# Subtracting the low parts of the first layer's converted weights on GpSimd instead of VectorE

## The chip, the cores and the metric

The kernel runs on one core of one Trainium2 chip. The metric is the device time of one execution in microseconds; the median of several executions is given. A core has five engines with a queue of their own each, and each queue is worked off in order: PE (TensorE, the matrix products), DVE (VectorE), ACT (ScalarE), POOL (GpSimd) and SP (SyncE, which here only issues DMAs). They wait for one another by semaphores. In the profile PEld stands for PE's weight loads.

## The reference

Three parts follow one another, all in float32:

```python
# 1: linear attention, q k v of (8, 8, 576, 64)
q_s = exp(q - max(q, -1)); q_s /= sum(q_s, -1) + 1e-9
k_s = exp(k - max(k, 2));  k_s /= sum(k_s, 2) + 1e-9
x = q_s @ (k_s^T @ v)                    # heads joined: 4608 x 512
# 2: first layer, moe_w_in 512 x 2048, moe_w_out 2048 x 512
x = (relu(x @ moe_w_in) ** 2) @ moe_w_out
# 3: second layer, moe2_w_in and moe2_w_out of the same shapes
h = x @ moe2_w_in
x = where(h > 0, h, exp(min(h, 0)) - 1) @ moe2_w_out
```

## The kernel before

**Split operands.** PE multiplies values of a rounded float type. To keep float32 accuracy each operand is split into a high part (the value, rounded) and a low part (the value minus its high part), and each product is made as three: high by high, high by low and low by high. For a weight tile of the first layer, the high part is made on ACT (`w_hi`, L133) and the low part is the subtraction of L143 (`w_lo`) on DVE.

**Conversion of the weights.** The weights come in as 64-bit words holding the float32 pairs and are taken apart by `w_scale` (two ACT instructions, L105 and L106) and put together by two bit operations on DVE, `w_fields` (L111) and `w_sign` (L116), into a tile `mt`, of which there are two. `w_hi` and `w_lo` then read `mt`. Each of these five steps works on one chunk, 128 x 512. The first layer has 32 chunks: wi0, tile 0 to 15, and wo0, tile 0 to 15, in the order in which they are used (the list `early`). Their high and low parts stay in SBUF (`resident` is true) in the tiles wi0h, wi0l and wo. The chunks of the second layer's wo1 are converted by the same functions with `resident` false, much later, and go to DRAM.

**Blocks.** The 4608 tokens are worked off in nine blocks of 512. Block 0 runs while the weights are converted: for each of the 16 tiles j, `up` (L544 to L546) makes twelve products for ph, ACT makes relu and square, ACT and DVE split the result into gh and gl (`up_split`, L565 on DVE), and `down` (L576 to L578) makes twelve products for y, two tiles behind. After each `up` come two calls of `convert(s, steps)`, one for each of 32 steps s. A call emits, in this order: `w_scale` for chunks up to s + 4; a third of the attention steps prepared for this s; `w_lo` up to chunk s + 1; a second third; `w_hi` up to s + 2 and `w_fields` up to s + 3; the last third; `w_sign` up to s + 3; and the load up to s + 8. The first three chunks' `w_lo` are emitted in `first_block`, which does the attention of block 0 in an order written out by hand.

**The attention steps beside it.** In the 32 steps of block 0 the attention of block 1 is done: for each of four pairs of heads, `k_max` (L259), `k_sub` (L272, one operand in PSUM), the exponential on ACT, `kv_mm` (the product pk, L286) and small sums on DVE; for each of four token tiles q, `q_max`, `q_sub` (L332), the exponential, `q_sum` and `q_norm` (L366). `x_tr` (L379) then transposes q on PE, and `x_mm` (L400) makes the block's input.

**POOL.** Its queue holds in these steps the memsets of the ones beside v (`v_load`, L249 and L250; vr has two buffers, so each waits for the pk product two pairs before) and of kvs (`kv_mm`, L295). Later it issues the DMAs that write the sums of the weights to DRAM (L199, L206, L211) and wo1's parts (L135, L145).

**Order.** All instructions are emitted in the order written in the code; nothing is reordered between emission and queue. The first layer's other eight blocks run in pairs with fewer products (L661, on sums of the weights prepared while blocks 1 and 2 run), and the second layer after them (L816, L877 to L879).

Of the kernel before, what the change touches and what calls it, by code (L numbers as in the profile page):

```python
# [13 lines left out]
ALU = mybir.AluOpType  # L14
# [6 lines left out]
def tile_attention_moe_moe2(  # L21
# [18 lines left out]
    nc = tc.nc  # L40
# [34 lines left out]
    def f32(ap):  # L75
        return ap.bitcast(F32)
# [3 lines left out]
    raw, mid, spill = {}, {}, {}  # L80
# [56 lines left out]
    def w_lo(w, j, resident):  # L137
        if resident:
            hi, lo = wh[w, j], wl[w, j]
        else:  # L140
            hi = spill.pop((w, j))
            lo = pool.tile([P, DM], F32R, tag="st", bufs=4, name=f"sl_{w}_{j}")
        nc.vector.tensor_tensor(lo, f32(mid.pop((w, j))), f32(hi), op=ALU.subtract)  # L143
        if not resident:
            nc.gpsimd.dma_start(w2d[w, j][:, 1, :], f32(lo))  # L145

# [322 lines left out]
    def first_block():  # L469
# [34 lines left out]
        for i, f in ((201, w_scale), (222, w_fields), (225, w_sign), (244, w_hi), (266, w_lo)):  # L504
            for c in range(-(-(325 - i) // 28)):
                put(i + 28 * c, chunk, f, c)
# [7 lines left out]
    def chunk(f, *cs):  # L514

        for c in cs:
            if 0 <= c < len(early) and (f, c) not in done:
                done.add((f, c))
                f(*early[c], *((True,) if f in (w_hi, w_lo) else ()))

    def convert(s, steps):


        i, j = len(steps) // 3, 2 * len(steps) // 3
        chunk(w_scale, *range(s + 5))
        run(steps[:i])
        chunk(w_lo, *range(s + 2))
        run(steps[i:j])
        chunk(w_hi, *range(s + 3))
        chunk(w_fields, *range(s + 4))  # L530
        run(steps[j:])
        chunk(w_sign, *range(s + 4))
        chunk(w_load, *range(s + 9))
# [728 lines left out]
```

## Time and profile before

| what | value |
|---|---|
| median of 3 timed runs | 1619.68 us (1619.37 to 1620.75) |
| span of the profiled execution | 1615.5 us |
| PE busy | 1586.3 us, 98% |
| DVE busy | 1051.3 us, 65% |
| ACT busy | 974.7 us, 60% |
| POOL busy | 90.6 us, 6% |
| granted clock of TensorE | 1.000, mean of the span |

The profile is of one execution. Its own time is the span from the first to the last instruction; the timed runs also hold what lies around it. Busy is the time in which an engine had an instruction under way; instructions of one engine can overlap at their ends, so a duration can be longer than the distance to the next start. The page's shares are means over the whole span; a change that touches one stage is read in the rows of that stage.

### The profile page before, as it was taken

The numbers are of one execution on the slowest core, as the hardware profiler recorded it, in microseconds if no ns is written. First come the engines' busy times: TensorE is split into PE (matmuls) and PEld (weight loads), VectorE is DVE, ScalarE is ACT, GpSimd is POOL, SyncE is SP. The second block draws the span as 40 slices with busy tenths as digits, with TensorE's granted clock in tenths as the row PEclk, the third lists the DMA queues.
The fourth block names the chain that finished last, engine by engine and source line by source line (L and its number), as shares of the span: only waits on it lengthen the run. The fifth ranks groups of instructions, "written<-read, shape, count | busy, mean of one in ns | idle before, by whom it ended". The sixth has DMA issues, their size and how long they took to land.

```text
span 1615.5 us, 22809 instructions
## 1 busy us (share of the span) xinstructions
PE 1586.3 (98%) x7958; PEld 1350.8 (84%) x7958; DVE 1051.3 (65%) x1658; ACT 974.7 (60%) x1665; POOL 90.6 (6%) x222
## 2 busy tenths in 40 slices
PE   6999999999999999999999999999999999999999
PEld 4778778878788787887888998998989999898997
DVE  7987596777877686773677554555545555555544
ACT  7996655566555675556556655555555565555544
POOL 0001220012101220011000000000000000000000
PEclk9999999999999999999999999999999999999999
DMA  7747566667775685653587555435534543543531
GB/s 264 258 156 246 197 216 198 204 210 237 257 226 174 219 289 164 201 196 111 181 288 259 197 194 173 150 110 154 171 106 143 172 129 117 190 125 109 172 112 59
DMA packets 163953, 296.17 MB, mean 183 GB/s; under 512 B 16384, under 2 KB 52224, under 8 KB 163840
## 3 DMA queue, kind: packets, MB, share of 16 engines
q1 hardware_dynamic: 154240, 263.25, 51.4%
q0 software_dynamic: 9600, 31.46, 4.9%
q8 instruction: 64, 1.05, 0.3%
q14 instruction: 49, 0.40, 0.1%
HBM read 238.03 MB, written 56.62 MB: 182 GB/s over the span
## 4 chain that ended last, share of the span: by engine, by line
PE 82%; DVE 8%; issue 5%; ACT 2%; DMA 2%; POOL 1%; SPq 1%; POOLq 0%; DVEq 0%; ACTq 0%
PE p L816 22%; PE p L661 18%; PE y L878 8%; PE y L879 8%; PE y L877 8%; PE ph L544 5%; PE ph L546 5%; PE ph L545 5%; PE px L400 2%; DVE ks L272 1%; PE pt L379 1%; PE pk L286 1%; DVE mt_wi L111 1%; DVE mt_wi L116 1%; POOL w1s L199 1%
## 5 line engine op out<-in xcount | busy, mean ns | idle before, releaser
L816 PE MATMUL p<-x2h,w 128*128 128x384 f32 x1344 | 359.6, 337 | 0.0
L661 PE MATMUL p<-uh,w 128*128 128x512 f32 x896 | 282.5, 392 | 2.9 <-DMA w<-w1s 2.9
L816 PEld LDWEIGHTS p<-x2h,w 128*128 128x128 f32 x1344 | 245.0, 188 | 4.4 <-ACT h L916 0.2
L544 PE MATMUL ph<-xh,wi0h 128*128 128x512 f32 x576 | 230.7, 401 | 0.1
L879 PE MATMUL y<-wo,g2l 128*128 128x512 f32 x576 | 226.0, 392 | 0.0
L878 PE MATMUL y<-wo,g2h 128*128 128x512 f32 x576 | 225.7, 392 | 0.0
L816 PE MATMUL p<-x2l,w 128*128 128x384 f32 x672 | 225.6, 336 | 0.0
L546 PE MATMUL ph<-xh,wi0l 128*128 128x512 f32 x576 | 225.0, 391 | 0.2 <-DVE wi0l L143 0.2
L545 PE MATMUL ph<-xl,wi0h 128*128 128x512 f32 x576 | 224.4, 390 | 0.0
L877 PE MATMUL y<-wo,g2h 128*128 128x512 f32 x576 | 224.0, 389 | 0.0
L661 PEld LDWEIGHTS p<-uh,w 128*128 128x128 f32 x896 | 168.2, 188 | 38.5 <-ACT uh L648 1.9
L918 DVE TENSOR_TENSOR h<-p,p 128x384 f32<-128x384 f32 x144 | 79.6, 553 | 183.1 <-PE p L816 181.9
L648 ACT ACTIVATE uh<-B 128x512 fp32r<-128x512 f32 x192 | 121.2, 632 | 109.4 <-PE p L661 63.7
L908 ACT ACTIVATE p<-p 128x384 f32<-128x384 f32 x144 | 69.9, 486 | 187.2 <-PE p L816 187.2
L649 DVE TENSOR_TENSOR ul<-B,uh 128x512 fp32r<-128x512 f32 x192 | 131.2, 690 | 69.3 <-ACT uh L648 68.3
L661 PE MATMUL p<-ul,w 128*128 128x512 f32 x448 | 175.3, 391 | 0.2
L553 ACT ACTIVATE B<-ph 128x512 f32<-128x512 f32 x128 | 76.2, 595 | 117.0 <-PE ph L546 116.4
L816 PEld LDWEIGHTS p<-x2l,w 128*128 128x128 f32 x672 | 126.2, 188 | 3.9
L544 PEld LDWEIGHTS ph<-xh,wi0h 128*128 128x128 f32 x576 | 109.2, 189 | 23.1 <-issue 0.9
L546 PEld LDWEIGHTS ph<-xh,wi0l 128*128 128x128 f32 x576 | 108.1, 188 | 24.1 <-DVE wi0l L143 1.1
L545 PEld LDWEIGHTS ph<-xl,wi0h 128*128 128x128 f32 x576 | 108.3, 188 | 22.8 <-issue 0.7
L879 PEld LDWEIGHTS y<-wo,g2l 128*128 128x128 f32 x576 | 108.1, 188 | 22.8
(127 smaller groups left out, 2372.1 us busy)
## 6 DMA issues: line engine op xcount, KB each, us to landing
w<-w2s SPq DMA_DIRECT2D x336, 256.0 KB, 3.0
w<-w1s SPq DMA_DIRECT2D x224, 256.0 KB, 3.4
raw_wi<-wi_dram SPq DMA_DIRECT2D x32, 512.0 KB, 4.2
raw_wo<-wo_dram SPq DMA_DIRECT2D x32, 512.0 KB, 4.0
ks<-k_dram SPq DMA_DIRECT2D x32, 320.0 KB, 4.7
vr<-v_dram SPq DMA_DIRECT2D x32, 320.0 KB, 5.6
kt<-kt_dram SPq DMA_DIRECT2D x32, 288.0 KB, 3.8
q<-q_dram SPq DMA_DIRECT2D x36, 256.0 KB, 4.7
```

What stands on the lines that cost most here:

```text
L544: nc.tensor.matmul(ph, hi[:, c], xh[p], start=(p == 0), stop=False)
L545: nc.tensor.matmul(ph, hi[:, c], xl[p], start=False, stop=False)
L546: nc.tensor.matmul(ph, lo[:, c], xh[p], start=False, stop=(p == NP - 1))
L553: nc.scalar.activation(g, ph, AF.Relu)
L648: nc.scalar.activation(hi, x, AF.Copy)
L649: nc.vector.tensor_tensor(lo, x, f32(hi), op=ALU.subtract)
L661: nc.tensor.matmul(accs[side, m], w[:, s, m], x, start=(new and (j, s) == (0, 0) and x is hi), stop=(j == NG - 1 and s == 1), skip_group_c ...
L816: nc.tensor.matmul(acc, w[:, s, k], x[:, k], start=(begin and (k, s) == (0, 0) and x is hi), stop=((k, s) == (1, 1)), skip_group_check=not ...
L877: nc.tensor.matmul(y2[c], gh[:, cs], hi, start=first, stop=False)
L878: nc.tensor.matmul(y2[c], gh[:, cs], lo, start=False, stop=False)
L879: nc.tensor.matmul(y2[c], gl[:, cs], hi, start=False, stop=last)
L918: nc.vector.tensor_tensor(h, part[add], part["bank", i], op=ALU.add)
```

## The change

In `w_lo` the subtraction goes to GpSimd where the parts are resident, which are the 32 chunks of wi0 and wo0, and stays on DVE for wo1's. Operands, tiles, their buffers and the place in the order of emission are the same.

```diff
@@ -140,7 +140,8 @@
         else:
             hi = spill.pop((w, j))
             lo = pool.tile([P, DM], F32R, tag="st", bufs=4, name=f"sl_{w}_{j}")
-        nc.vector.tensor_tensor(lo, f32(mid.pop((w, j))), f32(hi), op=ALU.subtract)
+        eng = nc.gpsimd if resident else nc.vector
+        eng.tensor_tensor(lo, f32(mid.pop((w, j))), f32(hi), op=ALU.subtract)
         if not resident:
             nc.gpsimd.dma_start(w2d[w, j][:, 1, :], f32(lo))
```

## Rows read from the trace of the kernel before

**Rows 1.** The page's first line: span and instructions.

```profile
span 1615.5 us, 22809 instructions
```

**Rows 2.** Instructions of L143: ns min/median/max, first and last start us, shapes.

```profile
L143 DVE TENSOR_TENSOR wi0l<-mt_wi,wi0h x16: 643/684/687, 25.2 to 115.8; 128x512 fp32r<-128x512 f32 x16
L143 DVE TENSOR_TENSOR wo<-mt_wo,wo x16: 679/685/692, 37.8 to 127.5; 128x512 fp32r<-128x512 f32 x16
```

**Rows 3.** Stretches: length, busy (count) of PE, PEld, DVE, ACT, POOL, clock, DMA share, GB/s.

```profile
41.00:61.00 20.00, 19.81 (x102) 15.40 (x101) 19.83 (x35) 18.89 (x36) 0.27 (x3) 1.00 0.73 257
61.00:81.00 20.00, 19.29 (x100) 15.05 (x100) 19.77 (x40) 17.82 (x35) 0.42 (x4) 1.00 0.75 254
81.00:101.00 20.00, 16.95 (x108) 13.32 (x106) 19.53 (x40) 18.76 (x37) 0.00 (x0) 1.00 0.44 145
101.00:121.00 20.00, 19.56 (x92) 15.86 (x93) 15.27 (x26) 18.80 (x36) 0.00 (x0) 1.00 0.48 166
...
140.00:238.00 98.00, 97.47 (x554) 78.54 (x554) 75.12 (x164) 62.19 (x121) 24.19 (x54) 1.00 0.69 237
```

**Rows 4.** Chain of waits, 20 to 145 us: start, length, engine, output, line.

```profile
59.83 0.61 DVE wi0l L143
...
61.80 0.69 DVE wo L143
...
65.55 0.60 DVE wi0l L143
...
68.81 0.60 DVE wo L143
...
100.78 0.61 DVE q L366
101.44 0.33 PE pt L379
```

**Rows 5.** DVE's groups, 41 to 101 us: busy us, mean ns, idle before.

```profile
L116 DVE SCALAR_TENSOR_TENSOR mt_wi<-raw_wi,mt_wi 128x512 int32<-128x512 int32 x10 | 6.9, 687 | 0.1
...
L143 DVE TENSOR_TENSOR wo<-mt_wo,wo 128x512 fp32r<-128x512 f32 x10 | 6.9, 686 | 0.0
L565 DVE TENSOR_TENSOR gl<-g,gh 128x512 fp32r<-128x512 f32 x10 | 6.9, 685 | 0.3 <-ACT gh L563 0.3
...
L143 DVE TENSOR_TENSOR wi0l<-mt_wi,wi0h 128x512 fp32r<-128x512 f32 x10 | 6.8, 680 | 0.0
L272 DVE TENSOR_TENSOR ks<-ks,pm 128x512 f32<-128x512 f32 (+1 forms) x8 | 3.5, 480 | 0.1
L366 DVE TENSOR_TENSOR q<-q,qz 128x512 f32<-128x512 f32 x4 | 2.7, 685 | 0.0
...
L353 DVE TENSOR_REDUCE qz<-q 128x8 f32<-128x512 f32 x4 | 2.7, 677 | 0.0
L259 DVE TENSOR_REDUCE km<-kt 128x1 f32<-128x576 f32 x3 | 2.2, 747 | 0.0
L327 DVE TENSOR_REDUCE qm<-q 128x8 f32<-128x512 f32 x3 | 2.0, 681 | 0.0
L362 DVE RECIPROCAL qz<-qz 128x8 f32<-128x8 f32 x4 | 0.8, 196 | 0.0
```

**Rows 6.** POOL's groups over the whole span, columns as in rows 5.

```profile
L295 POOL MEMSET kvs<- 128x128 f32 x32 | 6.7, 217 | 9.5 <-PE px L400 9.5
...
L249 POOL MEMSET vr<- 128x5 f32 x32 | 3.7, 118 | 175.7 <-PE pk L286 127.1 <-issue 48.6
...
masks.py:199 POOL TENSOR_SCALAR_AFFINE_SELECT ident<-ident 128x128 f32<-128x128 f32 x1 | 0.3, 288 | 0.1
```

**Rows 7.** Timeline near 60 us: start, us, instruction, idle before and releaser.

```profile
60.15 0.11 POOL L249 MEMSET vr<- 128x5 f32 x1 [38.35 <-PE pk L286]
...
62.59 0.61 ACT L133 ACTIVATE wi0h<-mt_wi 128x512 fp32r<-128x512 f32 x1
...
65.47 0.69 DVE L143 TENSOR_TENSOR wi0l<-mt_wi,wi0h 128x512 fp32r<-128x512 f32 x1
```

## The prediction

> **What bounds the kernel now.** The page comes first: the profiled execution has a span of 1615.5 us [rows 1], and the median of the three timed runs is 1619.68, so 4.2 us lie around the span. All sums below are made on the span and carried to the median by that difference. PE is the busiest engine over the whole, but the 32 instructions of the change start between 25.2 and 127.5 us [rows 2], so the page's averages say nothing about them and the stretches are read next.
>
> In the table of stretches [rows 3] the reader is to see three things. From 41 to 101 us DVE is busy 59.13 of 60 us (19.83 + 19.77 + 19.53). In the same 60 us PE is idle 3.95 (0.19 + 0.71 + 3.05) and ACT idle 4.53 (1.11 + 2.18 + 1.24): both are close behind. From 101 us DVE falls to 15.27 of 20 while PE is at 19.56, and from 140 to 238 PE is at 97.47 of 98. So there is one stretch that DVE sets, about 60 us long, and after it PE sets the time. The chain of waits cut to this part agrees [rows 4]: it goes from one DVE instruction to the next until the last query product ends and lets a PE transpose go at 101.44. Whatever DVE gains or loses before that moment moves PE, and with PE full afterwards it moves the end. A delay could still be absorbed where PE later waits for a weight load, but the preparation of that load is placed in the same step-by-step order as PE's work, so I count nothing for it.
>
> **What the change removes.** The line of the subtraction has 20 instructions in these 60 us, ten for wi0 and ten for wo0, with means of 680 and 686 ns [rows 5]. On the chain four of them in a row hold 0.61, 0.69, 0.60 and 0.60 us [rows 4], less than their duration, because the next one starts before the last has ended; the mean is 0.625. So 20 x 0.625 = 12.5 us leave the DVE queue. The other 12 leave DVE before 41 or after 101 us, where it has idle time (4.73 of 20 us from 101 to 121) and the chain goes by other engines; I count them at nothing, with 0.3 us either way at the start, where one stands between the first subtractions for x. If that cover were gone they too would be worth 0.625 each.
>
> **What it adds on GpSimd.** The trace before has no subtraction on POOL. Its rows are [rows 6]: a memset of 5 elements takes 118 ns, one of 128 elements 217, and the one instruction that reads a tile and writes one, 128 elements, 288. So writing costs (217 - 118) / 123 = 0.80 ns for each element, and reading one tile and writing 1.38. For 512 elements with one input that gives 118 + 507 x 1.38 = 0.82 us, a lower bound. A second input adds either another 0.58 or another 0.80 ns: 1.11 or 1.22 us. I take 1.11, an estimate from these three rows. Thirty-two of them are 36 us in a stretch of over 100 us in which POOL has next to nothing to do, so POOL doesn't become the bound by its own load.
>
> The latency is hidden too. A high part that ACT makes starts at 62.59 and takes 0.61, so it is there at 63.20; DVE comes to its subtraction only at 65.47, because its queue is late [rows 7]. POOL has no such queue and can end at about 64.3, before DVE would have begun. What newly waits is DVE's next bit assembly, two chunks later, because it writes the buffer that the subtraction reads (there are two of them); until now DVE's own order saw to that. It would be reached about 65.5 to 66, over a microsecond after the POOL subtraction is done. All of DVE is queued behind that wait, so this cover is lost if a POOL subtraction takes some 2.5 us.
>
> In POOL's queue the subtractions now stand among the memsets of vr and kvs. One of those held the queue for 38.35 us until the product pk at 60.15 [rows 7]. That looks dangerous but is only POOL's being far ahead: the memset is written two steps after the product that it waits for, and PE needs the low part behind it only five groups of products later. The DMA issues on POOL begin only after the last subtraction, and SP's copies of the wo0 weights wait for low parts that are long done. Cost: nothing.
>
> **What it costs DVE.** This term decides, and the trace doesn't have it: POOL never reads tiles beside DVE in this stretch, its memsets only write. From below, a POOL subtraction costs DVE nothing. From above, DVE stands still for all of it: 1.11 us, or 1.22. I take a value between: that a DVE instruction that itself reads two SBUF tiles stands still while POOL reads two, and that the others go on (reductions, the subtraction whose row comes from PSUM, the small ones). Of what is left to DVE in the 60 us, two tiles are read by the bit assemblies (four rows of 6.9 or 6.8, together 27.5), by gl (6.9) and by the two query products (2.7 each, 5.4): 39.8 us. The others are ks 3.5, the three reductions 2.7 + 2.2 + 2.0, and five small rows from 0.8 down that add up to 2.9: 13.3 us [rows 5]. The share that stands still is 39.8 / 53.1 = 0.75, so each POOL subtraction takes 0.75 x 1.11 = 0.83 us from DVE, 20 of them 16.6 us. Against the 12.5 us taken out this is +4.1 us: span 1619.6, median 1623.8.
>
> The memsets, the nearest rows for two engines at work, speak for no hindrance at all; but a memset reads nothing. The Trainium skill, page "SBUF — State Buffer", section "Who interferes with whom", says that a DVE instruction with two SBUF inputs contends with a GpSimd instruction that reads SBUF and not with one that only writes, and that the one that comes first keeps the shared pair for its whole instruction while the other "fully blocks". By that rule the change would come out as I take it, by no hindrance as in the first rival; no row of this trace bears the rule out or speaks against it.
>
> **The rivals.** *POOL works beside DVE for free; the sign turns.* DVE then needs 12.5 us less in the 60, and the next engine ends the gain: PE has 3.95 us of idle time to give back there and 0.44 up to 121 us, ACT 4.53. With all of PE's it is -4.4, with part of it (ACT has nearly the same work to do) about -3.5: 1616.2, down to 1615.3. It decides below a price of 0.625 us for each subtraction: there DVE gains. For it: DVE's hold on the chain is plain. Against it: two engines that read two whole tiles each.
>
> *DVE stands still for all of each POOL subtraction, or is made to wait for a late one.* 20 x 1.11 - 12.5 = +9.7: 1629.4; with 1.22 it is +11.9. For it: at a boundary between two instructions it is as likely as not a two-tile one that comes next. Against it: a quarter of DVE's time goes to instructions that read at most one tile.
>
> *The change moves the work and the time stays.* The price comes out near 0.625, or a saved wait is followed by the next one on ACT: 1619.7 within 1 us.
>
> **How the numbers follow.** A measurement of this kernel tells about 0.2%, 3.2 us, from no change. The forecast (price about 0.83, own range 1621 to 1627) has 0.38: slower by over 3.2 us with 0.24, within with 0.12, faster 0.02. Free work has 0.35: 0.27 faster by over 3.2, 0.08 within. Full standstill has 0.20: 0.18 slower, 0.02 within. The time that stays has 0.07: 0.06 within, 0.01 faster. Together faster 0.30, within 0.28, slower 0.42. The range takes in free work and most of the full standstill, 1615.5 to 1629; some 0.15 is left out, most of it above.
>
> **What would show it.** In the profile after: 32 subtractions on POOL at about 1.1 us each; if they take 2 us or more, they were themselves held. The bit assemblies on DVE, now 0.69 us: if some are 1.2 to 1.8 long, or idle time stands before them, DVE stands still; if all keep 0.69, the first rival holds. Then the moment at which PE's transpose for the last query tile goes, now 101.44: near 105.5 by the forecast, 97.5 to 98 by the first rival, 111 by the second. After it the distance to the end should be as it was. The prediction is wrong if that moment comes earlier, or if the time is made or lost after it.

## The result

The change makes the kernel slower: a median of 1630.0 us (1628.58 to 1631.55, 4 runs) against 1619.53 for the kernel before in runs beside it (1617.8 to 1620.75), a ratio of 1.0064 with a 95% interval of 1.0051 to 1.0076, or 8 to 12 us. The forecast was 1623.8 with a range up to 1629.0. The sign was right; the size was over twice the forecast's and lies above the range.

### The profile page after: what moved, and what is told of

The parts are those of the page before. It is cut to its first block, busy times and chain, and to the rows that moved or that the text cites. A ratio compares the mean times of both kernels' runs of the same rounds, so it can differ in the third digit from the quotient of the medians.

```text
span 1628.6 us, 22817 instructions
## 1 busy us (share of the span) xinstructions
PE 1589.9 (98%) x7958; PEld 1353.0 (83%) x7958; DVE 1051.4 (65%) x1626; ACT 975.1 (60%) x1665; POOL 141.7 (9%) x254
## 4 chain that ended last, share of the span: by engine, by line
PE 84%; DVE 6%; issue 4%; DMA 3%; ACT 2%; POOL 1%; SPq 0%; POOLq 0%; DVEq 0%; ACTq 0%
PE p L817 22%; PE p L662 17%; PE y L879 8%; PE y L880 8%; PE y L878 8%; PE ph L545 6%; PE ph L546 6%; PE ph L547 6%; PE px L401 2%; PE pt L380 1%; PE pk L287 1%; DVE mt_wi L111 1%; DMA kt<-kt_dram 1%; DVE mt_wi L116 1%; DMA w<-w1s 0%
## 5 line engine op out<-in xcount | busy, mean ns | idle before, releaser
L554 ACT ACTIVATE B<-ph 128x512 f32<-128x512 f32 x128 | 76.1, 594 | 117.0 <-PE ph L547 116.4
L547 PEld LDWEIGHTS ph<-xh,wi0l 128*128 128x128 f32 x576 | 108.9, 189 | 24.9 <-POOL wi0l L144 1.7
```

The costliest lines, as they stand in the source:

```text
L547: nc.tensor.matmul(ph, lo[:, c], xh[p], start=False, stop=(p == NP - 1))
L554: nc.scalar.activation(g, ph, AF.Relu)
```

## The profile after

The profiled execution took 1630.38 us with a span of 1628.6, so 1.8 us lie around the span. (The 4.2 us of the prediction were worked out from a profile and a median of different executions; the profiled execution of before was about 2 us faster than the median. Its mean granted clock was 1.000; of the 62 timed runs of the kernel before for which it is listed, nine show 1.000, 34 show 0.999 and 19 less.) In the kernel after, all lines behind L143 are one higher.

The subtractions on POOL, and what waits for them:

```profile
L144 POOL TENSOR_TENSOR wi0l<-mt_wi,wi0h x16: 1266/1637/3602, 25.5 to 123.7; 128x512 fp32r<-128x512 f32 x16
L144 POOL TENSOR_TENSOR wo<-mt_wo,wo x16: 1269/1428/2297, 38.0 to 133.0; 128x512 fp32r<-128x512 f32 x16
...
  DVE mt_wo L111: 5.0, 4
...
  DVE mt_wi L111: 1.2, 1
...
  PE ph L547: 0.6, 1
```

The shortest takes 1.27 us, where 1.11 was estimated; many take 1.6 to 1.8 and one 3.6. DVE now waits for them 6.2 us in five places. PE itself waits 0.6 us for a low part from POOL; in the kernel before it waited 0.5 us for low parts from DVE. The timeline of POOL, DVE and PE, merged in order of time from 83 to 109 us (start, length, instruction, idle before), shows what the long ones are:

```profile
83.77 1.29 POOL L144 TENSOR_TENSOR wo<-mt_wo,wo 128x512 fp32r<-128x512 f32 x1 [1.29 <-ACT wo L133]
...
83.98 1.63 DVE L111 SCALAR_TENSOR_TENSOR mt_wi<-raw_wi 128x512 int32<-128x512 int32 x1
...
87.82 1.64 POOL L144 TENSOR_TENSOR wi0l<-mt_wi,wi0h 128x512 fp32r<-128x512 f32 x1 [2.76 <-ACT wi0h L133]
...
88.25 1.24 DVE L359 TENSOR_SCALAR qz<-qz 128x8 f32<-128x8 f32 x1
...
90.83 2.30 POOL L144 TENSOR_TENSOR wo<-mt_wo,wo 128x512 fp32r<-128x512 f32 x1 [1.28 <-ACT wo L133]
...
91.28 0.67 DVE L367 TENSOR_TENSOR q<-q,qz 128x512 f32<-128x512 f32 x1
...
91.88 0.67 DVE L328 TENSOR_REDUCE qm<-q 128x8 f32<-128x512 f32 x1
...
92.48 1.19 DVE L116 SCALAR_TENSOR_TENSOR mt_wi<-raw_wi,mt_wi 128x512 int32<-128x512 int32 x1
...
94.20 0.68 DVE L333 TENSOR_TENSOR q<-q,qm 128x512 f32<-128x512 f32 x1
...
94.42 1.63 POOL L144 TENSOR_TENSOR wi0l<-mt_wi,wi0h 128x512 fp32r<-128x512 f32 x1 [1.15 <-ACT wi0h L133]
...
94.80 1.80 DVE L116 SCALAR_TENSOR_TENSOR mt_wo<-raw_wo,mt_wo 128x512 int32<-128x512 int32 x1
...
105.16 0.80 PE L287 MATMUL pk<-vr,ks 128*64 128x65 f32 x20 [3.17 <-ACT ks L278]
...
108.56 0.47 PE L380 MATMUL pt<-ident,q 128*128 128x128 f32 x1 [2.12 <-DVE q L367]
```

Read the pair at 94 us first. The POOL row that begins at 94.42 lasts until 96.05. The query subtraction, which reads two tiles, is at work on DVE until 94.88, so POOL's first 0.46 us are waiting, and 1.17 are left for the work. The next bit assembly on DVE should take 0.69 [rows 5] and takes 1.80: it ends at 96.60, 0.55 us after POOL. Each stood still for the other. At 83.77 POOL came first, and DVE's assembly ends 0.55 us after POOL's end again. At 90.83 POOL waits through the query product until 91.95; then the reduction at 91.88 runs beside it at its usual 0.67, and the assembly behind it is longer. So the split that the prediction assumed is there: rows that read two SBUF tiles stand still, the reduction and the subtraction from PSUM (ks, mean 478 ns after, 480 before [rows 5]) don't. One row was on the wrong side: the small addition of a constant at 88.25 has 8 elements and one tile, and takes 1.24 us in place of 0.16. The Trainium skill, page "SBUF — State Buffer", section "Who interferes with whom", gives both: two SBUF inputs on DVE contend with a GpSimd instruction that reads, and so does a one-input form in a two-port mode, under which it names the operation with a constant. The trace agrees with both (1.80 us for 0.69, 1.24 for 0.16); that the small row ran in such a mode, no run shows.

The table of stretches answers to [rows 3], with columns as there; its last three rows are shorter stretches between 102 and 110 us:

```profile
41.00:61.00 20.00, 18.69 (x80) 14.15 (x78) 19.52 (x27) 16.29 (x30) 10.70 (x9) 1.00 0.68 236
61.00:81.00 20.00, 17.07 (x107) 13.52 (x108) 18.71 (x29) 17.23 (x34) 11.12 (x13) 1.00 0.70 241
81.00:101.00 20.00, 18.39 (x99) 14.88 (x98) 19.77 (x32) 17.29 (x34) 9.87 (x9) 1.00 0.46 148
101.00:121.00 20.00, 14.71 (x76) 11.39 (x75) 14.00 (x22) 16.32 (x32) 9.24 (x7) 0.83 0.48 157
...
140.00:238.00 98.00, 97.47 (x555) 78.54 (x554) 70.83 (x157) 59.85 (x116) 22.73 (x51) 1.00 0.68 233
...
102.00:104.00 2.00, 0.00 (x0) 0.00 (x0) 2.00 (x3) 1.11 (x3) 1.70 (x1) 1.00 0.56 170
...
106.00:108.00 2.00, 0.44 (x3) 0.20 (x3) 0.79 (x2) 1.97 (x5) 1.31 (x2) 0.62 0.70 207
108.00:110.00 2.00, 1.44 (x4) 1.25 (x5) 1.95 (x3) 1.12 (x3) 1.32 (x1) 0.50 0.16 64
```

DVE is busy 58.0 of the 60 us, nearly as long as before, although 12.5 us of work have left it; PE is idle 5.85 us from 41 to 101, 1.9 more than before; and from 101 to 121 there is something new: PE is busy only 14.71 of 20 and its granted clock is 0.83. The chain of waits there, which answers to [rows 4]:

```profile
43.12 0.68 DVE gl L566
...
99.98 3.37 DMA raw_wo<-wo_dram
...
103.94 0.66 ACT raw_wo L106
104.60 0.71 ACT ks L278 x2
...
105.90 1.28 POOL wo L144
107.21 0.69 DVE mt_wo L111
107.90 0.61 DVE q L367
108.56 0.47 PE pt L380
109.03 0.43 PE ph L545
```

The transpose that the prediction named goes at 108.56, 7.1 us later than before (101.44), between the forecast's 105.5 and the second rival's 111. Two waits that the prediction had put at nothing stand on the way to it: DVE's late assemblies free a load buffer late (one ends at 99.91 and the load goes at 99.98), the load arrives late, and ACT stands at it in front of the exponential that PE needs for pk; and DVE waits at 107.21 for POOL's subtraction. PE's two rows at the end of the timeline say the same from their side: 3.17 us idle before pk, 2.12 before the transpose. After these waits the products come every 0.43 us instead of 0.23 for some 4 us: the clock was granted at 0.62 and then 0.50, which is the lower of its two levels. In the profile of the kernel before it was 1.00 in all these stretches.

The same gl that goes at 43.12 went at 41.37 in the chain of the kernel before:

```profile
41.37 0.69 DVE gl L565
```

Read as a ledger of the two traces, 1.7 us are lost before this point, 5.4 more until the transpose, and 2.2 behind it, where the clock is low. A measure that leaves out how early a run starts is block 0's length, from the first product for ph to the last for y, in the kernel before and then after (first and last start stand behind the durations; the rows for ph end at 240 us, where the view ends):

```profile
L544 PE MATMUL ph<-xh,wi0h x192: 389/389/792, 30.4 to 234.1; 128*128 128x512 f32 x192
L578 PE MATMUL y<-gh,wo x64: 388/389/504, 39.6 to 139.4; 128*128 128x512 f32 x64
```

```profile
L545 PE MATMUL ph<-xh,wi0h x187: 388/389/796, 30.5 to 240.0; 128*128 128x512 f32 x187
L579 PE MATMUL y<-gh,wo x64: 388/389/498, 40.0 to 148.7; 128*128 128x512 f32 x64
```

That is 109.0 us before and 118.2 after: +9.2, most of the 10.5 of the medians. From the last of these products to the end of the span it is 1476.1 us before and 1479.9 after, but 1476 to 1482 over the fourteen profiles of this case, so no single difference is read from that part; the section on the experiments returns to the clock in it.

## The experiments

Two theories stood against each other. **Standstill**: GpSimd's subtraction and DVE's two-tile instructions shut each other out. **Lateness**: GpSimd's results simply come later, and DVE (through the two buffers) and PE wait for them. The later runs ask what else is in the loss beside the standstill. Ratios are against runs of the kernel before on the same chip, with 95% intervals; block 0 is the length defined above, each from one profile.

| run | median us | ratio | block 0, us |
|---|---|---|---|
| before (profile of before) | 1618.49 to 1620.46 | 1 | 109.0 |
| the change | 1630.0 | 1.0064 (1.0051 to 1.0076) | 118.2 |
| two_tile_dummy | 1635.35 | 1.0086 (1.0070 to 1.0103) | 125.5 |
| one_tile_dummy | 1624.25 | 1.0022 (1.0011 to 1.0033) | 115.5 |
| write_only_dummy | 1619.08 | 0.9991 (0.9980 to 1.0002) | 108.9 |
| change_four_buffers | 1627.82 | 1.0046 (1.0028 to 1.0064) | 116.1 |
| ends_only | 1620.9 | 1.0001 (0.9992 to 1.0010) | 112.0 |
| middle_only | 1628.51 | 1.0045 (1.0030 to 1.0059) | 116.4 |
| half_wo_only | 1626.76 | 1.0035 (1.0023 to 1.0048) | 115.2 |
| change_pe_busy | 1634.33 | 1.0079 (1.0065 to 1.0093) | 122.4 |
| change_pe_fill | 1628.18 | 1.0055 (1.0041 to 1.0069) | 116.5 |
| change_fill_buffers | 1627.57 | 1.0053 (1.0040 to 1.0065) | 114.8 |
| middle_clean | 1626.89 | 1.0044 (1.0031 to 1.0057) | 113.2 |
| before_four_buffers | 1621.24 | 1.0011 (1.0003 to 1.0020) | 109.8 |

**Three kinds of idle work on GpSimd.** The subtraction of before stays, and behind it stands work for nobody, in a spare tile (each run has the lines that its name stands behind, and the line that makes the spare tile; in the third run a one-column copy makes the two memsets start when the others do):

```diff
         nc.vector.tensor_tensor(lo, f32(mid.pop((w, j))), f32(hi), op=ALU.subtract)
+        if resident:
+            spare = pool.tile([P, DM], F32, tag="st", bufs=4, name=f"spare_{w}_{j}")
+            nc.gpsimd.tensor_tensor(spare, f32(hi), f32(hi), op=ALU.subtract)   # two_tile_dummy
+            nc.gpsimd.tensor_copy(spare, f32(hi))                              # one_tile_dummy
+            nc.gpsimd.tensor_copy(spare[:, 0:1], f32(hi)[:, 0:1])              # write_only_dummy
+            nc.gpsimd.memset(spare, 0.0)                                       # write_only_dummy
+            nc.gpsimd.memset(spare, 0.0)                                       # write_only_dummy
```

> The low parts stay on VectorE; behind each of the 32, GpSimd makes a second subtraction of the high part from itself into a spare tile that nobody reads. Standstill (a GpSimd subtraction and a VectorE instruction that reads two tiles shut each other out): nothing is taken off VectorE, so the whole price of about 1.15 us for each of 20 shows: 1640 to 1645 us, and bit assemblies of 1.2 to 1.8 us in the profile. Rival, lateness (what cost time in the change is that VectorE and PE wait for results that GpSimd makes later): nobody waits for the spare tile, so 1618 to 1621 us and all VectorE rows at 0.69.

> As the run before, but GpSimd copies the high part into the spare tile, so it reads one tile. Standstill for any reading by GpSimd: a copy of about 0.8 us holds VectorE for 0.7 to 0.8 each, 20 of them: 1632 to 1637 us. If only two reading inputs on GpSimd shut VectorE out: 1618 to 1622. Lateness: 1618 to 1621.

> As the runs before, but GpSimd copies one column of the high part (so that it starts at the same moment) and then sets the spare tile to zero twice: about 1 us of GpSimd work that only writes. Standstill by reading: 1619 to 1622 us, VectorE rows at 0.69. If any work of GpSimd shuts VectorE out: 1632 or more. Lateness: 1618 to 1621.

The three rows of POOL, one from each kernel, wi0's half (ns min/median/max):

```profile
L146 POOL TENSOR_TENSOR spare_wi<-wi0h x16: 1040/1074/2697, 25.7 to 130.3; 128x512 f32<-128x512 f32 x16
```

```profile
L146 POOL COPY spare_wi<-wi0h x16: 610/616/1154, 25.1 to 119.5; 128x512 f32<-128x512 f32 x16
```

```profile
L147 POOL MEMSET spare_wi<- x16: 524/527/530, 25.4 to 113.9; 128x512 f32 x16
```

Lateness falls as the main cause: work whose result nobody waits for costs 11 to 17 us (by the interval of its ratio) when it reads two operands. The memsets cost nothing, and their row has no long instance at all: work that only writes meets no one. The copy lies between, near the low side: +4.5 us by the medians where 12 to 17 were expected of any reading. It takes 0.61 us alone, so it holds DVE for less, and DVE's longer rows add up to 6.8 us in its profile against 20.2 with the two operands (each row's excess over its usual length, 0.69 us, or 0.16 for the addition of a constant). The dummy subtraction's own price is thus about 0.6 us for each of 32, not the 1.15 that the expectation read from the change: the change's loss had more in it than standstill. (The dummy reads one tile twice and takes 1.04 us alone, where the change's subtraction of two tiles takes 1.27; it also writes another type, and no run tells the two apart.)

**Four buffers for the assembled words.**

```diff
-        mt = att.tile([P, DM], I32, tag="mt", bufs=2, name=f"mt_{w}_{j}")
+        home, tag, n = (pool, "st", 4) if w[2] == "0" else (att, "mt", 2)
+        mt = home.tile([P, DM], I32, tag=tag, bufs=n, name=f"mt_{w}_{j}")
```

> The change, with four buffers in place of two for the assembled words of the first layer, so that VectorE's next assembly need not wait for GpSimd's subtraction. Standstill: the 6.2 us of such waits go, but VectorE stands still in other places for most of it: 1626 to 1630 us. Lateness: most of the loss is gone, 1617 to 1621 us.

DVE's waits for POOL are gone from its profile, and block 0 is 2.1 us shorter than in the change. The medians agree in direction (1627.8 against 1630.0), but the runs overlap. The wait is a part of the loss, not its body.

**Which of the 32.** One more condition in the line of the change, with c the chunk's place in the order of use:

```diff
-        eng = nc.gpsimd if resident else nc.vector
+        eng = nc.gpsimd if resident and not 4 <= c < 24 else nc.vector   # ends_only
+        eng = nc.gpsimd if resident and 4 <= c < 24 else nc.vector       # middle_only
+        eng = nc.gpsimd if resident and w == "wo0" else nc.vector        # half_wo_only
```

> GpSimd subtracts only the first 4 and the last 8 of the 32 chunks, those outside the stretch from 41 to 101 us. Prediction's step (they cost nothing, 0.3 us either way): 1619 to 1620.5 us. Ledger read from the two traces (1.7 us are already lost at the start, before 43 us): 1620.5 to 1622.5 us, the loss made before 43 us.

> GpSimd subtracts only chunks 4 to 23, the 20 inside the stretch. Ledger: the change without its loss at the start, 8 to 9 us over before: 1627 to 1629 us, with the clock drop near 106 us still there. Prediction's sum for these 20 (standstill alone): 1623.8.

> GpSimd subtracts only wo0's 16 chunks, ten of them in the stretch. If each subtraction has its own price and they add up: half of the change's 10.5, 1624 to 1626 us. If the loss hangs on a threshold (PE kept waiting long enough for its clock to drop, VectorE's wait for a buffer): well under half, 1619 to 1622 us, with no clock drop in the profile.

The twelve outside the stretch cost nothing that the timed runs can tell; the 20 inside cost 5 to 10 us by themselves. So the stretch was rightly chosen. That the start loses 1.7 us, as the ledger had read, is not borne out by the median; block 0 of that one profile is 3.0 us longer, with a first product 1.2 us earlier and a drop of the clock (0.91 from 101 to 121 us), which shows how far one profile can stand from the median. Ten of the 20 (with six outside the stretch) cost 4 to 8 us, more than their half would be by the prediction's sum (2 us), and the clock in that profile fell to 0.83 from 101 to 121 us all the same. That range also holds half of the change's own loss (5.2), so the run doesn't show that the loss has a step.

**The clock.** Products that nobody reads, put where PE waits in the change; in the first form in a bank of their own, in the second in the bank of the next ph:

```diff
     def kv_mm(b, p):
+        if (b, p) == (1, 3):
+            fill_pe(12)          # change_pe_busy: 10, into bank([P, P], "busy")
...
     def x_tr(t, p):
+        if (t, p) == (1, 0):
+            fill_pe(8)           # change_pe_busy: 6
...
+    def fill_pe(n):
+        if not ahead:
+            ahead.append(psh.tile([P, TB], F32, tag="ph", name="ph0_0_12"))
+        for i in range(n):
+            nc.tensor.matmul(ahead[0][:, 0:P], ident, ident, start=True, stop=True)
```

> The change, with 10 idle products on PE before the last pk of block 1 and 6 before its first transpose, where PE waits 5 us in the change's profile; they fill waiting time. If the clock drop after that wait is a cost of its own (2.2 us in the ledger): the clock stays at 1.0 there and the time is 1627 to 1628.5 us. If the drop is only a sign of the wait: 1630 us or more.

> Like the run with idle products, but the 12 before pk and the 8 before the transpose now go into the bank of the next ph, which is free, so they wait for nothing (12 take 2.9 us and 8 take 1.9, by the run before; PE waits 3.2 and 2.1 there in the change). If the clock drop is a cost of its own: the clock is 1.0 from 101 to 121 us and the time is 1627 to 1628.5 us. If it is only a sign of the wait: 1630 us or more.

The first form tells nothing of the clock: its extra bank pushed the transposes onto one that ACT had yet to empty, and PE waited 4.5 us there. In the second the clock holds (first row: the change with fill; before it was 0.83):

```profile
101.00:121.00 20.00, 19.34 (x126) 16.36 (x125) 15.19 (x24) 17.83 (x35) 8.60 (x7) 1.00 0.52 174
```

Block 0 is 1.7 us shorter than in the change. The median is 1.8 us lower, as expected, but the runs overlap.

Longer waits of PE are not the only thing that goes with a drop of the clock. The run ends_only has no subtraction on POOL between 41 and 101 us, and its PE waits as in the kernel before, here before and then ends_only:

```profile
98.41 0.80 PE L286 MATMUL pk<-vr,ks 128*64 128x65 f32 x20 [1.09 <-issue]
...
101.44 0.33 PE L379 MATMUL pt<-ident,q 128*128 128x128 f32 x1 [1.75 <-DVE q L366]
```

```profile
98.66 0.80 PE L288 MATMUL pk<-vr,ks 128*64 128x65 f32 x20 [1.11 <-issue]
...
101.69 0.41 PE L381 MATMUL pt<-ident,q 128*128 128x128 f32 x1 [1.75 <-DVE q L368]
...
101.00:121.00 20.00, 19.30 (x84) 15.57 (x85) 12.80 (x20) 17.30 (x34) 8.86 (x6) 0.91 0.42 143
```

The clock stayed at 1.00 behind the first two waits and fell to 0.91 behind the second two. The deeper drop, to 0.83, is in all seven profiles in which these two waits together are longer and not filled, and in none of the three in which they are filled.

**Both, and then all of it.** change_fill_buffers has the four buffers with 12 and 4 idle products. middle_clean has the four buffers, GpSimd for chunks 4 to 23 alone, and 8, 10 and 4 idle products, the 8 before pair 0's pk, where another drop of the clock had shown (0.91 from 61 to 81 us in four of the profiles).

> The change with four buffers for the assembled words and with 12 and 4 idle products, so that both costs behind the standstill are taken away. Ledger: what is left is the start (1.7) and the standstill of the 20 (14.6 of longer VectorE rows against 12.5 taken out): 1623 to 1626 us. If the standstill alone makes the loss, both additions change little: 1628 to 1630 us.

> GpSimd subtracts chunks 4 to 23 only, with four buffers for the assembled words and with idle products on PE (8 before the first pk of block 1, 10 before the last, 4 before the first transpose) that fill its waits: the standstill of the 20 and nothing else. Prediction's term for these 20 (16.6 us of standstill against 12.5 taken out, +4.1): 1622.5 to 1625 us, clock 1.0 throughout, about 16 us of longer VectorE rows. If a cost not yet named is at work: 1626 to 1629 us.

Stretches of middle_clean:

```profile
41.00:61.00 20.00, 19.69 (x93) 15.87 (x93) 19.52 (x27) 16.87 (x32) 10.66 (x9) 1.00 0.67 241
61.00:81.00 20.00, 19.16 (x118) 15.11 (x118) 19.85 (x29) 18.15 (x36) 12.65 (x13) 1.00 0.73 244
81.00:101.00 20.00, 18.42 (x103) 15.05 (x102) 19.81 (x34) 17.09 (x33) 9.01 (x9) 1.00 0.45 152
101.00:121.00 20.00, 18.63 (x116) 15.40 (x116) 15.80 (x26) 18.16 (x35) 2.87 (x3) 1.00 0.52 174
```

and its last product for y:

```profile
L596 PE MATMUL y<-gh,wo x64: 388/389/504, 39.9 to 143.9; 128*128 128x512 f32 x64
```

In these four stretches the clock is 1.00. In DVE's timeline 20 rows, as many as there are subtractions, are 1.12 to 1.79 us long, with an excess of 17.3 us in all over their usual length; the prediction's term was 16.6. Against the 12.5 taken out that is +4.8, and block 0 is 4.2 us longer than before. So by the profile what was left in block 0 is about the prediction's term. The medians say more: both kernels miss what was expected, 1627.6 (1623 to 1626) and 1626.9 (1622.5 to 1625), with ratios that mean 5 to 11 us.

A part of the difference is in the clock behind block 0. The profile of middle_clean has two more drops there (first pair of rows), where the profile of the kernel before has none (second pair):

```profile
240.00:260.00 20.00, 18.11 (x74) 14.25 (x72) 15.30 (x20) 8.92 (x15) 0.00 (x0) 0.91 0.73 234
540.00:560.00 20.00, 17.95 (x96) 14.18 (x95) 12.84 (x30) 13.69 (x28) 7.29 (x12) 0.91 0.53 189
```

```profile
240.00:260.00 20.00, 19.48 (x105) 15.98 (x106) 14.93 (x24) 9.01 (x17) 0.14 (x2) 1.00 0.76 239
540.00:560.00 20.00, 19.47 (x95) 15.62 (x94) 8.19 (x15) 13.39 (x25) 4.92 (x7) 1.00 0.54 187
```

From its last product for y to its end it takes 1481.5 us, the longest of the fourteen, against 1476.1 in the kernel before. The timed runs point the same way. The one run of middle_clean with a mean granted clock of 1.000 took 1621.70 us, 3.2 to 3.8 more than the four runs of before with 1.000 on the same chip (1617.89 to 1618.47); its other five, at 0.997 and 0.998, took 1625.34 to 1628.99.

**The control.** The four buffers in the kernel before, all else as it was:

> The kernel before (all subtractions on VectorE) with the four buffers alone, the control for the runs with four buffers. If the buffers bring nothing by themselves: 1618.5 to 1620.5 us. If they loosen VectorE and ACT from one another: 1615 to 1618 us, which would beat both kernels.

They are no gain but a small loss, 0.5 to 3 us, with a drop of the clock (0.91 from 101 to 121 us) that the profile of the kernel before does not have. Measured against this control middle_clean loses 5.7 us by the medians and 3.4 by block 0. No run beat the kernel before, and none points to a version that would.

## Why the prediction was wrong

- **The stretch and what bounds it: right.** The 20 chunks from 41 to 101 us carry the loss, the other twelve none that can be timed (middle_only and ends_only).
- **That DVE's two-tile instructions stand still and the others go on: right.** The rows near 90 us show which stand still, and the three dummies that reading on POOL is what holds them. The one exception is the addition of a constant. POOL's own duration was estimated too low, 1.11 for 1.27.
- **The price for each subtraction, 0.83 us: right in size, in part by luck.** 20 long rows hold DVE for 17.3 us in middle_clean and for 17.7 in change_fill_buffers (41 to 109 us), against 16.6. Both factors were off, in opposite directions: with 1.27 in place of 1.11 the share of 0.75 would give 0.95 each, and the 17.3 us are 0.87 each, 0.68 of the 1.27. In the change itself 18 long rows add up to 15.7 between 41 and 109 us; that DVE could not be held where it was waiting already may be why, and is not shown.
- **What failed is the step "Cost: nothing" for everything behind the standstill**, in the paragraph on the latency and the buffer. (The one on the queues held: POOL's subtractions waited for nothing but ACT's high parts.) The margin of over a microsecond at DVE's next assembly was worked out for a POOL subtraction that starts at once and takes 1.11. It starts when DVE lets it and can take until 3.6, longer than the 2.5 us that the prediction itself gave as the end of that cover, and DVE waited 6.2 us. Taking that wait away shortens block 0 by 2.1 us. And time was made behind the transpose, 2.2 us, which the prediction had named as a sign of being wrong.
- **What the prediction doesn't have at all is the clock.** A DVE that is later makes ACT's exponential later, PE waits 3.2 and 2.1 us before pk and the transpose, and its next products run at the lower level. Filling the waits keeps the clock up and shortens block 0 by 1.7 us. Half of the change shows the same drop (0.83); a shallower one (0.91) comes without any longer wait, as in ends_only, so the clock of one profile is not the change's doing alone.
- By block 0 the ledger is then: +9.2 in the change, of which 3.4 go with buffers and fill, 1.6 more with the last drop of the clock and the twelve outer chunks, and 4.2 stay, the forecast's 4.1. By the medians the same steps are 10.5, 8.3 and 8.4: the first is borne out in direction, the second not.
- **What stays open.** By the medians the last two versions of the change lose 2 to 4 us more than block 0 accounts for. The drops of the clock behind block 0 and the one run of middle_clean at 1.000 (+3.2 to 3.8) fit each other, but that is one run, and the later drops are no mark of the change: write_only_dummy, which costs nothing, has one of 0.91 from 530 to 550 us, and so has before_four_buffers. Whether the change makes them more frequent, and why the clock holds behind a wait in one execution and falls behind the same wait in another, no run shows.

The second rival (1629.4) came nearest to the time, by luck: its sum lets DVE stand still for all of each subtraction, which the rows refute. Its other reason, that DVE is made to wait for a late result, is a part of the loss (6.2 us of waits), but no term of its sum.

## What to carry to other kernels

Before work is moved from VectorE to GpSimd, count how much of what VectorE keeps reads two SBUF tiles: about that share of GpSimd's time comes back as standstill, here 0.87 us for 0.625 saved. Of the three kinds of work tried here only the memsets, which write without reading, cost VectorE nothing. Where two engines run close behind the one that is slowed, its loss doesn't end with its own sum: price the waits that it hands on, and a matrix engine that is made to wait a few microseconds can be slower for a while afterwards.

## What was not expected of the hardware

A GpSimd subtraction of 128 x 512 takes 1.27 us in the change, with two tiles as operands, and 1.04 in the dummy, with the same tile twice and another type written; a copy takes 0.61 and a memset 0.53. A row's duration on either engine contains its waiting for the other (POOL 1.27 to 3.60, the bit assembly 0.69 to 1.84), so a long row is not slow work. An eight-element addition of a constant on VectorE was held like the large ones, 1.24 us for 0.16. The granted clock held at 1.00 behind PE's waits of 1.09 and 1.75 us in one profile and fell to 0.91 behind 1.11 and 1.75 in another.
